# Rows for the next expert as quarter rows turned by VectorE, against half rows turned by TensorE

## The chip, the cores and the metric

The kernel runs on one core of a Trainium2 chip. The metric is the device time of one execution in microseconds (us). The profile names the engines PE (TensorE, matmuls), PEld (TensorE's weight loads), DVE (VectorE), ACT (ScalarE), POOL (GpSimd) and SP (SyncE, which here issues DMAs).

## The reference

Sliding-window attention over 8 sequences of 576 tokens with 8 heads of 64 gives a matrix x of 4608 rows and 512 columns, in float32. A two-level gate then sends each row to one of 4 groups and to one of 4 experts in it, and every expert is a small two-layer network:

```python
xg = x[mask_g]                                   # rows of one group
h  = np.maximum(xg[mask_e] @ w1[g, e], 0.0)      # 512 -> 1024
ye = h @ w2[g, e]                                # 1024 -> 512
out[tok_idx] = combined[:, None] * ye            # gate weights of group and expert
```

So the attention's rows are sorted by expert, multiplied by two weight matrices, scaled, and written to their places in the output.

## The kernel before, in words

**Stages.** Up to some 180 us of the profile the attention runs (`scores`, `softexp`, `transpose_p`, `av`), writes its rows to a DRAM tensor `xd` (L378), and counts, per token, the expert and the slot in it (`route`). A table `tab` (L569) holds for every slot the gate weight and the indices of the row in `xd` and in `out`; an index is doubled there since a row is fetched in two halves. From about 209 us on only the experts' networks run, one "piece" after the other (L1132). Pieces come in the order of the experts' counts; their row counts are `PIECES` (L41): 186 and 150 for the two experts part of whose rows was already done during the attention (`EARLY`, function `early`), then 368, 302, 300, 298, 292, 284, 266, 264, 256, 256, 242, 238, 214, 188. A tile is 128 rows, so pieces 2 to 9 have three tiles and the others two.

**One piece.** `ffn` yields after every step k. Steps 0 to 7 are `layer1`: for each 128 of the 1024 hidden units twelve matmuls into one PSUM buffer `a` (weights and rows are each split into two float16 parts, high and low, and three of the four products are taken), then ACT writes `hh` = relu(a) as float16 (L795) and DVE the rest `hl` (L796). Four PSUM buffers turn for `a`. From step 8 on is `layer2`: for each tile 24 matmuls into `y` (L847), two steps per tile, then ACT scales y (L821, or L831 for a short tile, whose columns are dealt to groups of partitions) and GpSimd scatters the rows to `out` by an indirect DMA (L808). The short tile comes second. A matmul takes `hh` and `hl` of the hidden units in order, so the last `hl` is wanted for the 22nd of the first tile's 24.

**Weights.** They come as 512 KB chunks, eight per expert, issued by SP (L659) into seven staging buffers. `split` (L666) turns each into two float16 parts: ACT the high one (L673), DVE the low one (L670). Four chunks of the expert after the next are split in `layer2` of a piece, the other four in `layer1` of the piece that follows.

**Rows of the next piece.** This is what the change touches. At the head of piece i, `begin(i + 1)` calls `slots_of` (L1095): DVE picks the piece's indices out of `tab` (`select`, L722 and L729, then `unpack`, L693 to L695), and `gather` (L750) lets GpSimd issue two indirect DMAs per tile (L738), each fetching half a row for each of 128 partitions into a tile `xr` (five buffers). After the gathers stands one `nc.gpsimd.drain()` (L1137). (Piece 2's are asked for in piece 0, L1147.) In `layer2` of piece i, `between` calls `spread` (L761) for one tile of piece i + 1 at a time: TensorE makes four transposes into PSUM (L769), ACT copies that as float16 into `xh` (L770), DVE subtracts for `xl` (L771). The transposes stand in TensorE's queue between the matmuls of `layer2`:

```python
for c in range(4):
    nc.tensor.transpose(pt[:, c, 0:n], xr[0:n, c * P : c * P + P], id32[0:n, 0:n])
nc.scalar.copy(xh[:, :, t * P : t * P + n], pt[:, :, 0:n])
nc.vector.tensor_tensor(xl[...], pt[:, :, 0:n], xh[...], ALU.subtract)
```

**Order.** In the attention and in the experts alike the order of the instructions of PE, ACT and DVE is that in which the program writes them (`manual_schedule`), in the experts POOL's and SP's too; each engine takes its own in that order. Between the attention and the first piece the string `TAIL` (L54) deals out steps by hand: R and r are steps of the last `route`, w one of the weights' preparation, 0, 1 and 2 steps of the three `early` passes, B the first piece's slots and gathers, O a step of `order`, which ranks the experts. `overflow` (L1020) makes a list of rows that found no slot, in 14 steps of DVE, dealt out by `bgq` from piece 3 on.

Of the kernel before, what the change touches and what calls it, by code (L numbers as in the profile page):

```python
# [38 lines left out]
CAPS = (442, 406, 368, 302, 300, 298, 292, 284, 266, 264, 256, 256, 242, 238, 214, 188)  # L39
DONE = [max([o + n for q, o, n, _ in EARLY if q == r] + [0]) for r in range(len(CAPS))]  # L40
PIECES = [(r, DONE[r], n - DONE[r]) for r, n in enumerate(CAPS)]  # L41
CGR = TPB * P // 4
CMAX = max(n for _, _, n in PIECES)
MAXOV = 64
NEARLY = 2
SPLITS = (2, 0, 2, 2, 2, 2, 2, 1, 1, 1, 1)
DEEP = 3
NWST = 6
NWST2 = 1
BUDGET = (1.4, 1.4, 2.4, 1.8)  # L50
# [17 lines left out]
def moe_attention_kernel(ctx, tc, q, k, v, cmask, wgate, wpack, out):  # L68
# [135 lines left out]
    def setup(part):  # L204
        if part == 0:
            nc.vector.memset(ones, 1.0)
            nc.gpsimd.affine_select(
                out=upper, in_=ones, pattern=[[1, P]], compare_op=ALU.is_gt, fill=0.0, base=0, channel_multiplier=-1
            )
            nc.sync.dma_start(wgr, wgate)  # L210
            iota_of(pri, [[-1, 4]], 4, 0)
            iota_of(base[0], [[REG, NE]], 0, 0)
            iota_of(low, [[1, P]], 0, 0)
        if part == 1:
            iota_of(high, [[REG // P, NE], [1, NK4]], 0, 0)
            nc.vector.tensor_scalar(high, high, float(P), HUGE, ALU.mult, ALU.add)
            nc.scalar.copy(high_ps, high.rearrange("p e k -> p (e k)"))
            nc.scalar.copy(pri_ps, pri)
            nc.vector.memset(E16, 0.0)
            nc.vector.memset(tab[:, 0], 0.0)  # L220
            nc.vector.memset(tab[:, 1], 2.0 * NTOK)
            nc.vector.memset(tab[:, 2], 2.0 * NTOK + 1.0)
            ids = wgr[:, 128:].rearrange("p (h v t) -> p h t v", h=2, v=2)
            nc.vector.tensor_copy(val[:, :, 1:3], ids[:, 0])
            nc.vector.tensor_copy(parts[:, :, 1:3], ids[:, 1])
        if part == 2:
            nc.gpsimd.memset(xe[0][0], 0.0)
            nc.sync.dma_start(xd[NTOK : NTOK + 1, :], xe[0][0][0:1, :])
        if part == 3:
            for g, t in oob.items():  # L230
# [459 lines left out]

    def unpack(ent, cs, three):
        n = three.shape[-1]
        nc.vector.tensor_copy(ent[:, 1:3, 0:n], three[:, 1:3])  # L693
# [23 lines left out]
        nc.scalar.copy(csq, rp[:, 1:2])  # L717
        return entq, csq

    def select(ent, cs, which, k0, nt):  # L720
        sq = sm.tile([P, 3, nt, NE], F32, name=f"sel{nt}")
        nc.vector.tensor_tensor(  # L722
            sq,
            tab[:, :, :, k0 : k0 + nt].rearrange("p v e k -> p v k e"),
            which.unsqueeze(1).unsqueeze(2).broadcast_to([P, 3, nt, NE]),
            ALU.mult,
        )
        three = sm.tile([P, 3, nt], F32, name=f"three{nt}")
        nc.vector.tensor_reduce(three, sq, axis=AX.X, op=ALU.add)  # L729
        unpack(ent, cs, three)  # L730
        return three

    def new_slots():
        return fs.tile([P, 3, 4], I32, name="sent"), fs.tile([P, 4], F32, name="cs")
# [15 lines left out]
    def gather(ent, cap):  # L750
        xrs = []
        for t, n in tiles(cap):
            xr = rows.tile([P, 512], F32, name="xr", bufs=5)
            fetch_rows(xr, ent, t)
            xrs.append(xr)
        return xrs

    def new_x(pl, cap=CMAX):
# [16 lines left out]
    more_a = [psS]  # L775

    def new_a():
        more_a.append(more_a.pop(0))
# [233 lines left out]
    def take(shape):  # L1012
# [4 lines left out]
        t = spare[:, lo : lo + n]  # L1017
        return t.rearrange("p (a b) -> p a b", a=shape[0]) if len(shape) > 1 else t

    def overflow():  # L1020
        T = lambda nm, shape: take(shape)
        cnt = T("cnt", [NE])
# [72 lines left out]
    def slots_of(i):  # L1095
        r, off, cap = pieces[i]
        ent, cs = new_slots()
        three = select(ent, cs, top[:, r] if r < NEARLY else perm[:, r], off // P, nt(cap))
        tq = note_tail(cs, three, cap)
        return ent, cs, gather(ent, cap), tq  # L1100

    def begin(i, got=None):
        ent, cs, xrs, tq = got or slots_of(i)
        return ent, cs, xrs, new_x(fx), tq

    cur = []

    def first(k):
        if 0 < k <= nt(pieces[0][2]):
            spread(cur[3], cur[2], pieces[0][2], (k - 1,))  # L1110

    def ready():
        cur[:] = begin(0)
# [5 lines left out]
    step = dict(R=lambda: part(lastr), r=lambda: run(lastr), w=lambda: run(wq), B=ready, O=lambda: run(rq))  # L1119
    step.update((str(i), lambda q=q: run(q)) for i, q in enumerate(eb))  # L1120
    for c in TAIL:
        step[c]()
# [5 lines left out]
    yq = [take([DM // 2]) for _ in range(2)]  # L1128
    for t in yq:
        nc.gpsimd.memset(t, 0.0)  # L1130
    ahead, sooner = [], []
    for i, (r, off, cap) in enumerate(pieces):  # L1132
        more = i + 1 < len(pieces)
        if more:
            nxt = begin(i + 1, sooner.pop() if sooner else None)
            ncap = pieces[i + 1][2]
            nc.gpsimd.drain()  # L1137
        nsel = nt(cap)

        def between(k):  # L1140
            m, d = nt(ncap), 2 * nsel - 2
            if more and k < d:
                spread(nxt[3], nxt[2], ncap, range(m * k // d, m * (k + 1) // d))
# [16 lines left out]
        if more:  # L1160
            cur = nxt
    run(bgq, 100)

    nov = nc.values_load(ovn[0:1, 0:1], min_val=0, max_val=MAXOV)
# [26 lines left out]
def layout(q, k, v, moe_w_group, moe_w_expert, moe_w1, moe_w2):  # L1191
# [70 lines left out]
```

## Time and profile before

| | us |
|---|---|
| three runs | 580.63, 582.28, 584.22 |
| median of them | 582.28 |
| the profiled execution | 584.71 |
| its span, first to last instruction | 583.0 |
| from the first matmul of piece 0 to the first of piece 15 | 351.34 |

The trace belongs to the profiled execution, which took 2.43 us more than the median. A stretch of it is named by its start and end in us from the span's start. "Busy" of PE is modelled, since matmuls are pipelined; where PE is called busy all the time, the distance from one matmul's start to the next one's tells what it costs. DVE's and ACT's durations overlap by some 0.07 us where two instructions follow each other at once.

### The profile page before, as it was taken

The numbers are of one execution on the slowest core, as the hardware profiler recorded it, in microseconds if no ns is written. First come the engines' busy times: TensorE is split into PE (matmuls) and PEld (weight loads), VectorE is DVE, ScalarE is ACT, GpSimd is POOL, SyncE is SP. The second block draws the span as 40 slices with busy tenths as digits, with TensorE's granted clock in tenths as the row PEclk, the third lists the DMA queues.
The fourth block names the chain that finished last, engine by engine and source line by source line (L and its number), as shares of the span: only waits on it lengthen the run. The fifth ranks groups of instructions, "written<-read, shape, count | busy, mean of one in ns | idle before, by whom it ended". The sixth has DMA issues, their size and how long they took to land.

```text
span 583.0 us, 16256 instructions
## 1 busy us (share of the span) xinstructions
PE 553.9 (95%) x6460; PEld 396.0 (68%) x6460; DVE 386.1 (66%) x801; ACT 331.4 (57%) x656; POOL 248.5 (43%) x275
## 2 busy tenths in 40 slices
PE   3989999897899999999999999999999999999995
PEld 2777877675767777656666666675766766776873
DVE  5756987889688636855877876565655756756720
ACT  7456685865766427744455555555466656555521
POOL 2885675647464342342343425151541422332411
PEclk9899999999799999999999999999999999999999
DMA  7999898993772176875667566576856767867210
GB/s 236 347 295 294 297 289 260 313 326 102 245 264 91 56 290 217 264 254 166 195 206 229 188 203 216 188 240 202 267 185 225 241 229 234 277 221 247 82 30 31
DMA packets 45344, 127.41 MB, mean 219 GB/s; under 512 B 6845, under 2 KB 7747, under 8 KB 45266
## 3 DMA queue, kind: packets, MB, share of 16 engines
q1 hardware_dynamic: 37506, 105.36, 56.2%
q0 software_dynamic: 7760, 20.99, 10.2%
q8 instruction: 52, 0.85, 0.6%
q14 instruction: 26, 0.21, 0.1%
HBM read 107.44 MB, written 19.22 MB: 217 GB/s over the span
## 4 chain that ended last, share of the span: by engine, by line
PE 69%; issue 2%; DVE 1%; DMA 1%; POOL 1%; ACT 1%; POOLq 0%; SPq 0%
PE y L847 32%; PE a L788 31%; PE pt L769 3%; DMA w<-wpack 1%; DVE mv L534 0%; PE o L331 0%; PE lt_ps L406 0%; PE tx L392 0%; POOL out L808 0%; PE rp L714 0%; PE bank L553 0%; POOL xe L979 0%; DVE wa2l L670 0%; POOL vs L152 0%; ACT wa2h L673 0%
## 5 line engine op out<-in xcount | busy, mean ns | idle before, releaser
L738 POOL DMA_INDIRECT xr<-xd,sent x80 | 95.2, 1190 | 32.6 <-issue 21.5
L808 POOL DMA_INDIRECT out<-yr,sent x30 | 30.9, 1029 | 179.4 <-ACT yr L821 148.5
L847 PEld LDWEIGHTS <-hh 128*128 128x128 f16 (+14 forms) x960 | 67.1, 99 | 57.7 <-issue 2.7
L796 DVE SCALAR_TENSOR_TENSOR hl<-a,hh 128x256 f16<-128x256 f32 (+14 forms) x136 | 56.9, 421 | 62.6 <-ACT hh L795 62.5
L795 ACT ACTIVATE hh<-a 128x256 f16<-128x256 f32 (+14 forms) x136 | 51.5, 383 | 49.7 <-PE a L788 49.0
L788 PE MATMUL a<-xh,wb1h 128*128 128x256 f16 (+7 forms) x288 | 76.7, 270 | 0.0
L788 PE MATMUL a<-xh,wb1l 128*128 128x256 f16 (+7 forms) x288 | 76.6, 270 | 0.0
L788 PE MATMUL a<-xl,wb1h 128*128 128x256 f16 (+7 forms) x288 | 76.6, 270 | 0.0
L771 DVE TENSOR_TENSOR xl<-pt,xh 128x512 f16<-128x512 f32 (+14 forms) x42 | 24.6, 589 | 74.2 <-ACT xh L770 74.2
L821 ACT ACTIVATE yr<-y,cs 128x512 f32<-128x512 f32 (+4 forms) x30 | 20.6, 687 | 88.9 <-PE y L847 59.6
L788 PE MATMUL a<-xh,wa1h 128*128 128x186 f16 (+7 forms) x256 | 70.8, 277 | 0.0
L788 PE MATMUL a<-xh,wa1l 128*128 128x186 f16 (+7 forms) x256 | 70.7, 277 | 0.0
L788 PE MATMUL a<-xl,wa1h 128*128 128x186 f16 (+7 forms) x256 | 70.7, 277 | 0.0
L788 PEld LDWEIGHTS <-wa1h 128*128 128x128 f16 x640 | 59.6, 99 | 11.6 <-issue 0.5
L788 PEld LDWEIGHTS <-wb1h 128*128 128x128 f16 x576 | 54.2, 98 | 9.6 <-issue 0.2
L847 PE MATMUL y<-wb2h,hh 128*128 128x512 f16 (+7 forms) x272 | 59.7, 305 | 0.0
L847 PE MATMUL y<-wb2l,hh 128*128 128x512 f16 (+7 forms) x272 | 59.6, 304 | 0.0
L847 PE MATMUL y<-wb2h,hl 128*128 128x512 f16 (+7 forms) x272 | 59.5, 304 | 0.0
L847 PE MATMUL y<-wa2h,hh 128*128 128x512 f16 (+7 forms) x208 | 56.8, 331 | 0.0
L847 PE MATMUL y<-wa2h,hl 128*128 128x512 f16 (+7 forms) x208 | 56.6, 330 | 0.0
L847 PE MATMUL y<-wa2l,hh 128*128 128x512 f16 (+7 forms) x208 | 56.6, 330 | 0.0
L148 POOL TENSOR_SCALAR vs<-v 64x1040 f32<-64x1040 f32 x36 | 38.7, 1088 | 30.2 <-DMA v<-v 18.5
(206 smaller groups left out, 1255.0 us busy)
## 6 DMA issues: line engine op xcount, KB each, us to landing
w<-wpack SPq DMA_DIRECT2D x128, 512.0 KB, 4.1
v<-v SPq DMA_DIRECT2D x36, 260.0 KB, 5.5
kr<-k SPq DMA_DIRECT2D x34, 256.0 KB, 5.4
qb<-q SPq DMA_DIRECT2D x17, 512.0 KB, 6.0
xd<-x SPq DMA_DIRECT2D x32, 256.0 KB, 4.3
xr<-xd,sent POOLq DMA_INDIRECT x80, 4.1
xd<-x SPq DMA_DIRECT2D x8, 128.0 KB, 4.0
qb<-q SPq DMA_DIRECT2D x2, 256.0 KB, 2.8
```

Source lines behind the costliest of these rows:

```text
L148: nc.gpsimd.tensor_scalar(vs[n][even], vt[n][even], 1.0, 1.0, ALU.mult, ALU.mult)
L738: nc.gpsimd.indirect_dma_start(out=xr[:, 256 * h : 256 * h + 256], out_offset=None, in_=xd[0:known].rearrange("n (h c) -> (n h) c", h=2), ...
L769: nc.tensor.transpose(pt[:, c, 0:n], xr[0:n, c * P : c * P + P], id32[0:n, 0:n])
L771: nc.vector.tensor_tensor(xl[:, :, t * P : t * P + n], pt[:, :, 0:n], xh[:, :, t * P : t * P + n], ALU.subtract)
L788: nc.tensor.matmul(a[:, 0:cap], ww[:, c * FF + f * P : c * FF + f * P + P], xx[:, c, 0:cap], start=(i == 0), stop=(i == len(mm) - 1),)
L795: nc.scalar.activation(hh[:, f, 0:cap], a[:, 0:cap], AF.Relu)
L796: nc.vector.scalar_tensor_tensor(hl[:, f, 0:cap], a[:, 0:cap], 0.0, hh[:, f, 0:cap], ALU.max, ALU.subtract)
L808: ins = nc.gpsimd.indirect_dma_start(out=out.rearrange("n (g c) -> (n g) c", g=g), out_offset=bass.IndirectOffsetOnAxis(ap=at, axis=0), in ...
L821: nc.scalar.activation(yr[0:n, :], yp[0:n, :], AF.Copy, scale=cs[0:n, t : t + 1])
L847: nc.tensor.matmul(yp[P // g * j : P // g * j + n, 0 : DM // g], h[:, f, t * P : t * P + n], ww[:, f * DM + DM // g * j : f * DM + DM // g ...
```

## The change

Each row of `xd` is now seen as four quarters of 128 columns. For 32 rows of a tile, one indirect DMA fetches all four quarters: partitions 32j to 32j + 31 receive quarter j of the 32 rows. A full tile takes four such DMAs, a shorter one as many as it has groups of 32 rows. DVE then turns 32x32 blocks (`spread_quarters`) into a tile `xt` in SBUF, and ACT and DVE make `xh` and `xl` from it. With this the row's column 4p + c stands on partition p in chunk c, so the first weight matrix is laid out anew on the host, and the tiles that TensorE still transposes (the `early` ones and piece 0) read every fourth column.

The quarter rows' indices come from a second table, made once by sixteen small matmuls and one DVE instruction (`quarter_table`, Q in `TAIL`); `quarter_rows` picks a piece's indices from it. A tile at a time is asked for, at every odd step, as long as fewer than five tiles are held, up to three pieces ahead (`ask_ahead`); G and H in `TAIL` ask for piece 1 and for the first tile of piece 2. The turns come at steps 3, 5, 7 and 9. The DRAIN stands at step 5. `overflow` gets only steps divisible by four.

```diff
-    "R0rw00rrrrrrrrrrrw1rrrr0rr1r1rr11rrr1rrB1w12w1ww112w22ww2w2O2O2O2O2O2O"
-    "222"
+    "R0rw00rrrrrrrrrrrw1rrrr0rr1r1rr11rrr1rrB1w1Q2w1Gww112w22ww2w2O2O2O2O2O2O"
+    "222H"
...
+    def quarter_table():
+        ps = new_a()[:, 0 : 4 * NE * NK4].rearrange("p (t n) -> p t n", t=4)
+        for T in range(4):
+            for j in range(4):
+                nc.tensor.matmul(
+                    ps[Q4 * j : Q4 * j + Q4, T],
+                    id32[:, Q4 * T : Q4 * T + Q4],
+                    tab[:, 1 + j // 2].rearrange("p e k -> p (e k)"),
+                    start=True,
+                    stop=True,
+                )
+        tabq.append(take([4, NE * NK4]))
+        nc.vector.tensor_scalar(tabq[0], ps, 2.0, odd, ALU.mult, ALU.add)
+
+    def quarter_rows(which, k0, nt):
+        sq = qsq[:, 0 : 4 * nt * NE].rearrange("p (k t e) -> p k t e", k=nt, t=4)
+        nc.vector.tensor_tensor(
+            sq,
+            tabq[0].rearrange("p t (e k) -> p k t e", k=NK4)[:, k0 : k0 + nt],
+            which.unsqueeze(1).unsqueeze(2).broadcast_to([P, nt, 4, NE]),
+            ALU.mult,
+        )
+        at = qat[:, 0 : 4 * nt].rearrange("p (k t) -> p k t", k=nt)
+        nc.vector.tensor_reduce(at, sq, axis=AX.X, op=ALU.add)
+        entq = fs.tile([P, 4, 4], I32, name="sentq")
+        nc.vector.tensor_copy(entq[:, 0:nt], at)
+        return entq
...
+    def gather_quarters(entq, cap, xrs):
+        def tile_of(t, n):
+            xr = rows.tile([P, 4, P], F32, name="xr", bufs=NXR)
+            for T in range((n + Q4 - 1) // Q4):
+                nc.gpsimd.indirect_dma_start(
+                    out=xr[:, T],
+                    out_offset=None,
+                    in_=xd.rearrange("n (g c) -> (n g) c", g=4),
+                    in_offset=bass.IndirectOffsetOnAxis(ap=entq[:, t, T : T + 1], axis=0),
...
+    def spread_quarters(xs, xrs, cap):
+        turned = []
+        for t, n in tiles(cap):
+            m = (n + Q4 - 1) // Q4
+            xt = rows.tile([P, 4, 4, Q4], F32, name="xt")[:, 0:m]
+            nc.vector.transpose(xt, xrs[t][:, 0:m].rearrange("p t (d c) -> p t c d", c=4))
+            held_rows[0] -= 1
+            turned.append((t, m, xt))
+            if t:
+                halves_of(xs, *turned.pop(0))
+            yield
+        halves_of(xs, *turned.pop(0))
+        yield
+
+    def halves_of(xs, t, m, xt):
+        xt = xt.rearrange("p t c j -> p c t j")
+        h, l = (x[:, :, t * P : t * P + m * Q4].rearrange("p c (t j) -> p c t j", j=Q4) for x in xs)
+        nc.scalar.copy(h, xt)
+        nc.vector.tensor_tensor(l, xt, h, ALU.subtract)
...
+            xq = xr.rearrange("p (d c) -> p c d", c=4)
             for c in range(4):
-                nc.tensor.transpose(pt[:, c, 0:n], xr[0:n, c * P : c * P + P], id32[0:n, 0:n])
+                nc.tensor.transpose(pt[:, c, 0:n], xq[0:n, c], id32[0:n, 0:n])
...
+    def ask_ahead(i):
+        if held_rows[0] < NXR:
+            if known[-1][4]:
+                ask(1, known[-1])
+            elif len(known) < min(i + 4, len(pieces)):
+                known_next(1)
...
-        more = i + 1 < len(pieces)
-        if more:
-            nxt = begin(i + 1, sooner.pop() if sooner else None)
-            ncap = pieces[i + 1][2]
-            nc.gpsimd.drain()
+        nxt, turn = None, []
+        if i + 1 < len(pieces):
+            while known[i + 1][4]:
+                ask(1, known[i + 1])
+            nxt = begin(known[i + 1])
+            turn = [spread_quarters(nxt[3], nxt[2], pieces[i + 1][2])]
         nsel = nt(cap)
-
-        def between(k):
-            m, d = nt(ncap), 2 * nsel - 2
-            if more and k < d:
-                spread(nxt[3], nxt[2], ncap, range(m * k // d, m * (k + 1) // d))
-
-        for k, _ in enumerate(ffn(wsets[r % 2], cur[3], cur[0], cur[1], cap, new_h, between, cur[4])):
-            if i == 0 and k == 1:
-                sooner.append(slots_of(2))
+        for k, _ in enumerate(ffn(wsets[r % 2], cur[3], cur[0], cur[1], cap, new_h, tq=cur[4])):
+            if k % 2:
+                ask_ahead(i)
+                if k == 5:
+                    nc.gpsimd.drain()
+                if k > 2:
+                    run(turn)
...
-            elif r > NEARLY:
+            elif r > NEARLY and k % 4 == 0:
                 run(bgq)
...
-    w1 = np.asarray(moe_w1).reshape(NE, 4, P, FF).transpose(0, 2, 1, 3).reshape(NE, P, 4 * FF)
+    w1 = np.asarray(moe_w1).reshape(NE, P, 4 * FF)
```

## Rows read from the trace of the kernel before

**Rows 1.** The page, busy time of the engines over the span.

```profile
PE 553.9 (95%) x6460; PEld 396.0 (68%) x6460; DVE 386.1 (66%) x801; ACT 331.4 (57%) x656; POOL 248.5 (43%) x275
```

**Rows 2.** The chain of work that ended last, 209.16 to 560.50 us, by line.

```profile
by line: PE y L847 48.8%; PE a L788 46.0%; PE pt L769 4.8%; PE rp L714 0.5%
```

**Rows 3.** Busy time by stretch: all pieces but the last, piece 1, piece 8.

```profile
core 0: us, PE busy (x) PEld busy (x) DVE busy (x) ACT busy (x) POOL busy (x), PEclk, DMA share, GB/s
209.16:560.50 351.34, 351.34 (x2967) 239.47 (x2966) 227.58 (x424) 196.65 (x334) 125.01 (x110) 1.00 0.67 217
...
225.86:240.31 14.45, 14.45 (x237) 11.31 (x237) 10.76 (x19) 11.25 (x22) 2.00 (x2) 1.00 0.92 301
...
406.44:430.97 24.53, 24.53 (x262) 16.61 (x261) 15.06 (x28) 14.48 (x26) 10.80 (x9) 1.00 0.69 227
```

**Rows 4.** Timeline of PE in piece 4: start, duration, instruction, count.

```profile
317.16 0.38 PE L847 MATMUL y<-wa2l,hh 128*128 128x512 f16 x1
317.38 0.60 PE L769 MATMUL pt<-id,xr 128*128 128x128 f32 x4
317.91 0.29 PE L847 MATMUL y<-wa2h,hh 128*44 128x256 f16 x2
...
319.13 0.27 PE L847 MATMUL y<-wa2l,hh 128*44 128x256 f16 x2
319.33 0.66 PE L769 MATMUL pt<-id,xr 128*128 128x128 f32 x4
319.92 0.29 PE L847 MATMUL y<-wa2h,hh 128*44 128x256 f16 x2
...
321.13 0.28 PE L847 MATMUL y<-wa2l,hh 128*44 128x256 f16 x2
321.34 0.44 PE L769 MATMUL pt<-id,xr 42*128 42x42 f32 x4
321.71 0.39 PE L847 MATMUL y<-wa2h,hh 128*128 128x512 f16 x1
```

**Rows 5.** DVE's groups by shape: count, busy us, mean ns, idle before.

```profile
L670 DVE SCALAR_TENSOR_TENSOR wb2l<-w,wb2h 128x1024 f16<-128x1024 f32 x32 | 38.8, 1216 | 0.0
...
L771 DVE TENSOR_TENSOR xl<-pt,xh 128x512 f16<-128x512 f32 x28 | 19.2, 689 | 56.9 <-ACT xh L770 56.9
...
L796 DVE SCALAR_TENSOR_TENSOR hl<-a,hh 128x266 f16<-128x266 f32 x8 | 3.4, 431 | 3.7 <-ACT hh L795 3.7
...
L722 DVE TENSOR_TENSOR sel<-tab,perm 128x144 f32<-128x144 f32 x8 | 3.2, 405 | 0.0
...
L796 DVE SCALAR_TENSOR_TENSOR hl<-a,hh 128x150 f16<-128x150 f32 x8 | 2.2, 306 | 1.3 <-ACT hh L795 1.3
...
L722 DVE TENSOR_TENSOR sel<-tab,perm 128x96 f32<-128x96 f32 x6 | 1.9, 319 | 0.0
...
L722 DVE TENSOR_TENSOR sel<-tab,top 128x48 f32<-128x48 f32 x2 | 0.5, 230 | 0.0
```

**Rows 6.** TensorE, transposes' weight loads (ns), and a row of the chain.

```profile
L769 PEld LDWEIGHTS pt<-id,xr x160: 133/140/143, 202.7 to 554.9; 128*128 128x128 f32 x104, 58*128 58x128 f32 x4, 22*128 22x128 f32 x4, 112*128 112x128 f32 x4
...
158.26 1.02 PE o L331 x32
```

**Rows 7.** Gathers and scatters: groups, landing, and two gathers beside one DVE instruction.

```profile
L738 POOL DMA_INDIRECT xr<-xd,sent x80: 992/1044/2052, 180.8 to 547.9; - x80
...
DMA to landing us min/median/max: 2.7/4.1/6.3
...
L808 POOL DMA_INDIRECT out<-yr,sent x30 | 30.9, 1029 | 179.4 <-ACT yr L821 148.5 <-ACT xh L770 15.2 <-DVE tq L706 4.3
...
306.13 1.00 POOL L738 DMA_INDIRECT xr<-xd,sent  x1 [0.30 <-issue]
307.44 1.64 POOL L738 DMA_INDIRECT xr<-xd,sent  x1 [0.30 <-issue]
...
306.99 1.22 DVE L670 SCALAR_TENSOR_TENSOR wb2l<-w,wb2h 128x1024 f16<-128x1024 f32 x1
```

**Rows 8.** Timeline of DVE at the end of piece 1.

```profile
239.33 1.22 DVE L771 TENSOR_TENSOR xl<-pt,xh 128x512 f16<-128x512 f32 x2 [2.44 <-ACT xh L770]
```

More of the change, by code (lines that the diff above doesn't have):

```diff
@@ L41 @@
 PIECES = [(r, DONE[r], n - DONE[r]) for r, n in enumerate(CAPS)]
+Q4 = P // 4
 CGR = TPB * P // 4
@@ L47 @@
 DEEP = 3
+NXR = 5
 NWST = 6
@@ L184, in moe_attention_kernel @@
     capt = cp.tile([P, NE], F32, name="capt")
+    odd = cp.tile([P, 1], F32, name="odd")
     top = cp.tile([P, NEARLY, NE], F32, name="top")
@@ L692, in unpack @@
         n = three.shape[-1]
-        nc.vector.tensor_copy(ent[:, 1:3, 0:n], three[:, 1:3])
+        if three.shape[1] == 3:
+            nc.vector.tensor_copy(ent[:, 1:3, 0:n], three[:, 1:3])
         nc.vector.tensor_scalar(ent[:, 0, 0:n], three[:, 1], 0.5, 0.0, ALU.mult, ALU.add)
@@ L718, in tail_slots, with select @@
         return entq, csq
-    def select(ent, cs, which, k0, nt):
-        sq = sm.tile([P, 3, nt, NE], F32, name=f"sel{nt}")
+    def select(ent, cs, which, k0, nt, nv=3):
+        sq = sm.tile([P, 3, nt, NE], F32, name=f"sel{nt}")[:, 0:nv]
         nc.vector.tensor_tensor(
             sq,
-            tab[:, :, :, k0 : k0 + nt].rearrange("p v e k -> p v k e"),
-            which.unsqueeze(1).unsqueeze(2).broadcast_to([P, 3, nt, NE]),
+            tab[:, 0:nv, :, k0 : k0 + nt].rearrange("p v e k -> p v k e"),
+            which.unsqueeze(1).unsqueeze(2).broadcast_to([P, nv, nt, NE]),
             ALU.mult,
         )
-        three = sm.tile([P, 3, nt], F32, name=f"three{nt}")
+        three = sm.tile([P, 3, nt], F32, name=f"three{nt}")[:, 0:nv]
         nc.vector.tensor_reduce(three, sq, axis=AX.X, op=ALU.add)
@@ L752, in gather @@
         for t, n in tiles(cap):
-            xr = rows.tile([P, 512], F32, name="xr", bufs=5)
+            xr = rows.tile([P, 512], F32, name="xr", bufs=NXR)
             fetch_rows(xr, ent, t)
@@ L756, in gather, with new_x @@
         return xrs
-    def new_x(pl, cap=CMAX):
+    def gather_quarters(entq, cap, xrs):
[7 more added lines that the diff above has]
+                    in_offset=bass.IndirectOffsetOnAxis(ap=entq[:, t, T : T + 1], axis=0),
+                    bounds_check=4 * NTOK + 3,
+                    oob_is_err=False,
+                )
+            xrs.append(xr)
+        return [lambda t=t, n=n: tile_of(t, n) for t, n in tiles(cap)]
+    def spread_quarters(xs, xrs, cap):
[16 more added lines that the diff above has]
+        nc.vector.tensor_tensor(l, xt, h, ALU.subtract)
+    def new_x(pl, cap=(CMAX + Q4 - 1) // Q4 * Q4):
         return pl.tile([P, 4, cap], F16, name="xh"), pl.tile([P, 4, cap], F16, name="xl")
@@ L1018, in take @@
         return t.rearrange("p (a b) -> p a b", a=shape[0]) if len(shape) > 1 else t
+    qsq, qat = take([4 * 3 * NE]), take([4 * 3])
     def overflow():
@@ L1097, in slots_of, with ask, begin, known_next @@
         ent, cs = new_slots()
[L1098 to L1103, printed above, removed]
-        return ent, cs, xrs, new_x(fx), tq
+        which = top[:, r] if r < NEARLY else perm[:, r]
+        xrs, asks = [], []
+        if i:
+            asks = gather_quarters(quarter_rows(which, off // P, nt(cap)), cap, xrs)
+            three = select(ent, cs, which, off // P, nt(cap), 2)
+        else:
+            three = select(ent, cs, which, off // P, nt(cap))
+            xrs = gather(ent, cap)
+        return ent, cs, xrs, note_tail(cs, three, cap), asks
+    def ask(n, got):
+        for _ in range(min(n, len(got[4]))):
+            got[4].pop(0)()
+            held_rows[0] += 1
+    def begin(got):
+        ent, cs, xrs, tq, _ = got
+        return ent, cs, xrs, new_x(fx), tq
+    known = []
+    def known_next(n):
+        known.append(slots_of(len(known)))
+        ask(n, known[-1])
+    def ask_ahead(i):
[4 more added lines that the diff above has]
+                known_next(1)
     cur = []
@@ L1110, in first @@
             spread(cur[3], cur[2], pieces[0][2], (k - 1,))
+            held_rows[0] -= 1
     def ready():
-        cur[:] = begin(0)
+        known.append(slots_of(0))
+        held_rows[0] = nt(pieces[0][2])
+        cur[:] = begin(known[0])
     lastr = [route(NBP - 1)]
@@ L1118, in moe_attention_kernel @@
     eb.append([early(2, new_x(fx), new_h, first)])
-    step = dict(R=lambda: part(lastr), r=lambda: run(lastr), w=lambda: run(wq), B=ready, O=lambda: run(rq))
+    step = dict(R=lambda: part(lastr), r=lambda: run(lastr), w=lambda: run(wq), B=ready, O=lambda: run(rq), Q=quarter_table)
+    step.update(G=lambda: known_next(9), H=lambda: known_next(1))
     step.update((str(i), lambda q=q: run(q)) for i, q in enumerate(eb))
@@ L1157, in moe_attention_kernel @@
                 todo.pop(0)()
-            elif r > NEARLY:
+            elif r > NEARLY and k % 4 == 0:
                 run(bgq)
-        if more:
-            cur = nxt
+        while run(turn, 9):
+            pass
+        cur = nxt
     run(bgq, 100)
```

7 lines of the change are left out of this document (5 added, 2 removed).

## The prediction

> **What bounds the kernel now.** I read the page's busy times first, then the chain of waits of the experts' stretch, then stretches, then single instructions. On the page PE is busy 95% of the span, DVE 66%, ACT 57%, POOL 43% [rows 1]. An average over two different stages says little, so: from the first matmul of piece 0 to the first of piece 15 PE is busy all of 351.34 us, at a granted clock of 1.00, DVE 227.58 (65%), POOL 125.01 (36%), and the 16 DMA engines 0.67 [rows 3]. The chain there holds PE alone: layer 2 48.8%, layer 1 46.0%, the transposes of the next piece's rows 4.8% [rows 2]. No other engine's wait ends last. So in this stretch one us of TensorE's time taken away is one us gained, as long as what replaces it keeps up.
>
> **What the change removes.** The transposes of pieces 1 to 15: two tiles for piece 1, three each for pieces 2 to 9, two each for 10 to 15, so 38 tiles. The chain's share gives 0.048 x 351.34 = 16.9 us [rows 2], 0.44 per tile. Starts of matmuls show the whole price. A 512-column matmul takes 0.216 (512 columns at the 2.4 GHz level); with the transposes between, the next starts 317.91 - 317.16 = 0.75 later, so they cost 0.53. The second set costs 0.79 - 0.11 = 0.68, the third, of 42 rows, 0.58 - 0.11 = 0.47 [rows 4]; 1.68 for a piece where the chain counts 0.53 + 0.59 + 0.37 = 1.49. The difference is time that the chain books on the matmul before a transpose. By that ratio 16.9 becomes about 19.0. I take 18.0, between 16.9 and 19.0.
>
> **What it adds on TensorE.** (a) Sixteen matmuls of 64 columns with 32 output partitions, after the table is done. The nearest row: 32 float32 matmuls of that width and 130 columns take 1.02 us, four side by side [rows 6]; sixteen are 0.5. Below: 0.25 by columns. Above: one after another at a transposes' set's 0.53 per four, 2.1. I take 0.5. (b) The transposes that stay (four early tiles, two of piece 0, 24 weight loads) now read every fourth column, 16 bytes apart. No row shows TensorE reading so. Below: nothing. Above: as DVE's strided read, priced next, 0.7 x 0.140 [rows 6] x 24 = 2.4. I take the middle, 1.2.
>
> **What it adds on DVE.** No row shows a 32x32 turn. Contiguous rows: 512 elements take 689 ns, 266 take 431, so 1.05 ns per element and some 0.15 us besides [rows 5]. L722 reads its table at a step of 16 bytes: 48, 96 and 144 elements take 230, 319 and 405 ns, so 1.8 ns per element [rows 5]. The turn reads at the same step. A full tile thus takes 0.69 to 1.07 us; I take the upper end, since the access is the same. Groups of 32 rows: piece 1 has 5, piece 2 has 12, pieces 3 to 6 have 10 each, 7 to 9 have 9 each, 10 to 13 have 8 each, 14 has 7, 15 has 6: 129, or 16,512 elements. At 1.8 ns that is 30 us, with 0.15 for each of 38 tiles 35; at 1.05, 23.
>
> The Trainium skill weighs on this: its page "SBUF — State Buffer", section "Door 1: The DMA port swizzle", says that SBUF is read in 16-byte lines and that each access that goes to a new line pays. L722 agrees (1.8 against 1.05) [rows 5]. The page does not say which engine pays; if TensorE's weight loads do, its rule gives the 2.4 us of (b) and 1.2 us more than my sum, if not, 1.2 less.
>
> The index pick per piece grows: a product of 192 elements instead of 144 (0.5 against 0.4), a reduction and a cast more, a third of the old select less: some 0.7 us, 10 for 15 pieces. `xl`'s subtraction reads SBUF instead of PSUM with the same count, so 0.69 as before [rows 5]. DVE's 227.58 becomes 261 to 273 of some 333 us, 82% at most: it is not the bound over the stretch.
>
> Inside a piece it can be. Piece 8 (266 rows): layer 1 takes eight times 12 x 0.113 = 10.9 us, and the last `hl` is wanted after 21 more matmuls of 0.216, 15.4 us from the start. In DVE's queue up to it stand 8 `hl` (0.36 from start to start), four weight splits (1.14), a step of the overflow list (1.4), two turns (0.6 to 1.0) and one subtraction (0.6): 10.7 to 11.5, from 1.8 us on, done at 12.5 to 13.3. There are 2 us to spare, and four buffers of `a` let DVE lag by three steps before.
>
> Piece 1 is the tight one: 150 rows, 14.45 us with 0.43 + 0.91 of transposes in it, 13.1 without, and piece 2's three long tiles to be made ready in it. Already in the run before, the third `xl` ends at 239.33 + 1.22 = 240.55 [rows 8], as piece 2 begins at 240.31 [rows 3]. Then DVE has up to that point 8 `hl` (0.25 from start to start; 0.306 each alone [rows 5]) 2.0, five splits 5.7, three turns 2.0 to 3.2, three subtractions 1.8, and piece 4's index pick 1.6: 13.1 to 14.3, from 1.2 us on, so it ends at 14.3 to 15.5. TensorE waits 1.2 to 2.4 us, once. I take 1.8. With nothing in front (DVE idle, pick later) it is 0; with a turn at twice my price 5.
>
> **What it moves.** GpSimd: 76 gathers become 129, each of 128 pieces of 512 bytes, 8.5 MB instead of 10.0. A gather takes 1.04 us (0.99 to 2.05) and 0.30 passes to the next; a scatter 1.03 [rows 7]. A piece with ten gathers and three scatters: 13 x 1.34 = 17.4 us of 25.5; if all gathers meet a DVE split (1.64 instead of 1.00 [rows 7]) 23.4 of 25.5. Each tile is asked for at least some eight steps before its turn, over 10 us, and lands in 4.1 [rows 7]. Queued behind a gather are the scatters; with two buffers of `y` rows one may be some 10 us late before ACT waits. The DRAIN stands behind a gather before and after; nothing visible waits for it, so 0. On DMA, 16,512 pieces instead of 9,728 make at most a few hundredths on 0.67 [rows 3]. ACT copies from SBUF instead of PSUM, the same count: 0. The overflow list's steps come later, beside matmuls: 0.
>
> **The sum**, against the profiled execution's 584.7: -18.0 + 0.5 + 1.2 + 1.8 = -14.5, so 570.2. The median of the runs shown is 2.4 below that execution, so 567.8, **568 us**, 2.5% faster. Ends of its terms: -19.0 + 0.25 + 0 + 0 gives 563.5, and -16.9 + 2.1 + 2.4 + 5 gives 574.9.
>
> **Rivals.** (1) DVE gives part back in every piece: a turn waits for its gather or takes 2 us instead of 1, and `hl` comes late. The margin in piece 8 is 2 us, so turns of 2.1 use it up; a wait of 0.6 us beyond it in each of 13 pieces makes 568 + 8 = 576. For: the turn is in no row. Against: 2 us of margin. (2) The turn is so slow that DVE is the bound: that needs 333 - 227.6 - 10 = 95 us for 38 tiles, 2.5 us each, over twice the strided price; near it, stalls give most of 18 us back: 582. (3) Slower: POOL becomes the bound. In the stretch there are 36 scatters at 1.33 and some 120 gathers. It would be as long as today at (351 - 48) / 120 = 2.52 us per gather, its 0.30 included; that is the point from which it decides. The longest row is 2.05 + 0.30 = 2.35. If each gather met two of DVE's two-input instructions, 1.00 + 2 x 0.64 + 0.30 = 2.58, and the requests of a piece also stood one us behind the turn that frees their buffer, 15 x 1 + 120 x 2.58 + 48 = 373, 22 us over today's 351: 604. For: the change makes `xl` another instruction with two SBUF inputs. Against: the median gather is at 1.04.
>
> The Trainium skill backs the third's mechanism: "SBUF — State Buffer", section "Who interferes with whom", has such a DVE instruction and a GpSimd one that reads SBUF exclude each other. The trace agrees, 1.64 beside a split against 1.00 [rows 7].
>
> (4) The change doesn't do what it says: the transposes go, but something else ends last already, as a weight chunk. Against: no such wait in the chain [rows 2]; DMA at 0.92 in piece 1 [rows 3] for it. Then 580.
>
> **How the numbers follow.** The forecast 0.70, (1) 0.14, (2) 0.05, (3) 0.07, (4) 0.04. About 1% can be told from no change, that is 576.5 and 588.1. Faster by over 1%: 0.70 and 0.11 of (1), 0.81. Within: 0.03 of (1), 0.05 of (2), 0.04 of (4) and 0.01 of (3), 0.13. Slower by over 1%: 0.06 of (3). For eight in ten I take the forecast from a little below its low end, 562.5, and most of (1), up to 577.5.
>
> **What would show it.** Right: L769 with 24 instead of 176 matmuls; PE busy without a gap from piece to piece but for one of 1 to 2.4 us before piece 2; piece 4's length shorter by 1.7 us; turns of 0.7 to 1.1 us per tile; gathers still near 1.0 to 1.7 us; POOL's busy share under 65% in the stretch. Wrong: matmuls of layer 2 waiting for L796, or of layer 1 for `xl`, in every piece; turns above 2 us; gathers above 2.2 us; a fall of the granted clock where such gaps stand.

## The result and the profile after

The changed kernel takes 586.6 us (median of 12 runs, 583.56 to 589.05), the kernel before in the same session 582.22 (579.85 to 584.22). The ratio is 1.0073, with a 95% interval of 1.0050 to 1.0096: a little slower, by some 4 us, where 568 had been forecast. The profiled execution took 587.25 us, its span is 585.5.

The page of the changed kernel: busy times, then the granted clock in 40 slices, then the chain that ended last, by engine.

```profile
PE 542.3 (93%) x6340; PEld 381.8 (65%) x6340; DVE 425.6 (73%) x870; ACT 332.2 (57%) x656; POOL 329.5 (56%) x332
...
PEclk9999999999999999789999999999998999999999
...
PE 53%; issue 6%; DVE 6%; DMA 4%; POOL 3%; ACT 2%; POOLq 1%; SPq 0%; DVEq 0%; ACTq 0%
```

Against [rows 1], PE has 120 instructions fewer and is busy 11.6 us less, but in a span that is 2.5 us longer. TensorE no longer bounds every stretch: in the chain of the experts' stretch, which held PE alone before [rows 2], DVE, DMA and POOL now appear. The clock dips at 234 to 263 us and at 439 to 454, in a stretch where it was 1.00 before [rows 3].

Stretches of the changed kernel, the counterparts of [rows 3]: all pieces but the last; piece 1; piece 2. The columns are as there.

```profile
207.28:563.50 356.22, 339.19 (x2813) 225.25 (x2812) 264.70 (x485) 197.57 (x334) 202.68 (x162) 0.98 0.65 211
...
223.29:246.12 22.83, 13.55 (x226) 10.02 (x225) 14.20 (x30) 10.99 (x22) 13.27 (x13) 0.91 0.59 188
246.12:280.33 34.21, 33.02 (x168) 17.96 (x168) 24.24 (x36) 17.38 (x27) 22.10 (x17) 0.91 0.68 211
```

The stretch is 356.22 us instead of 351.34, and TensorE idles in 17.0 of it. Piece 1 alone took 14.5 before; now it takes 22.83, with TensorE busy 13.55. By pieces, from the start of each one's first matmul in the two timelines of PE:

| pieces | before, us | after, us | difference |
|---|---|---|---|
| 0 | 16.80 | 16.01 | -0.8 |
| 1 | 14.52 | 22.83 | +8.3 |
| 2 | 31.99 | 34.21 | +2.2 |
| 3 to 7, together | 133.97 | 126.49 | -7.5 |
| 8 | 24.54 | 24.29 | -0.3 |
| 9 | 24.08 | 28.60 | +4.5 |
| 10 to 14, together | 105.44 | 103.79 | -1.7 |

(In [rows 3] the window of piece 1 begins 0.07 us after its first matmul, hence 14.45 there.) So where nothing stops TensorE, the gain is there: 1.5 us in each of pieces 3 to 7. It is given back in pieces 1, 2 and 9, and in smaller parts in 8, 11 and 12: in run 5 below, where nothing stops TensorE there, piece 8 takes 23.06 us and pieces 10 to 14 together 101.24.

The turns and gathers themselves, the changed kernel's groups by line (count, busy us, mean ns, idle before) and the weight loads of the transposes that stayed (shortest, median, longest ns):

```profile
L798 POOL DMA_INDIRECT xr<-xd,sentq x124 | 152.8, 1232 | 93.3 <-issue 38.7 <-DVE sel L728 22.8 <-DVE xT L764 6.1
...
L815 DVE STREAM_TRANSPOSE xt<-xr 128x512 f32<-128x512 f32 (+3 forms) x38 | 36.6, 962 | 0.0
...
L842 PEld LDWEIGHTS pt<-id,xr x8: 192/209/214, 200.7 to 204.4; 128*128 128x128 f32 x4, 58*128 58x128 f32 x4
```

What stops TensorE is to be read at the end of piece 1, backwards from PE. Four timelines of the changed kernel (start, duration, engine, line; in brackets the idle time before and what ended it). PE:

```profile
236.84 0.27 PE L920 MATMUL y<-wb2l,hh 128*22 128x128 f16 x4
246.12 0.47 PE L861 MATMUL a<-xh,wa1h 128*128 128x368 f16 x1 [9.01 <-ACT xh L827]
247.78 0.47 PE L861 MATMUL a<-xl,wa1h 128*128 128x368 f16 x1 [1.19 <-DVE xl L828]
```

ACT, with the end of piece 0's first tile and the copy that PE waits for:

```profile
220.70 0.69 ACT L894 ACTIVATE yr<-y,cs 128x512 f32<-128x512 f32 x1 [2.85 <-issue]
...
245.45 0.62 ACT L827 CAST xh<-xt 128x512 f16<-128x512 f32 x1 [9.13 <-DVE xt L815]
```

DVE:

```profile
236.28 0.25 DVE L735 TENSOR_REDUCE three<-sel 128x6 f32<-128x96 f32 x1
243.89 0.17 DVE L700 TENSOR_SCALAR sent<-three 128x3 int32<-128x3 f32 x1 [7.36 <-DMA out<-yr,sent]
...
244.34 1.08 DVE L815 STREAM_TRANSPOSE xt<-xr 128x512 f32<-128x512 f32 x1
```

POOL:

```profile
227.37 1.03 POOL L798 DMA_INDIRECT xr<-xd,sentq  x1 [0.30 <-issue]
228.71 1.00 POOL L798 DMA_INDIRECT xr<-xd,sentq  x1 [0.30 <-issue]
235.80 0.99 POOL L798 DMA_INDIRECT xr<-xd,sentq  x1 [6.09 <-DVE xT L764]
...
239.70 1.00 POOL L798 DMA_INDIRECT xr<-xd,sentq  x1 [0.30 <-issue]
241.00 1.03 POOL L881 DMA_INDIRECT out<-yr,sent  x1 [0.31 <-issue]
```

Read from the end: the first matmul of piece 2 waits for `xh`, that for the third turn, and the turn stands in DVE's queue behind L700. L700 writes the slot table `sent` of piece 4. The pool of tables has four buffers, and with the look-ahead of the change five pieces are known in piece 1, so the buffer is that of piece 0, which its scatter still reads. That scatter's data were ready at 220.70 + 0.69 = 221.39, but it was issued at 241.00: 19.6 us late. In that time GpSimd did what stood in front of it in its queue, ten gathers, and idled 6.1 us once. The profile puts the end of this idle time down to DVE. Another row of the same trace, the one for the line of the DRAIN, says otherwise (sequencer, count, shortest, median, longest ns, first and last start), for the window 215 to 228 us:

```profile
L1247 POOLq DRAIN  x1: 13743/13743/13743, 221.2 to 221.2; - x1
```

From 221.2 to 234.9 the sequencer sits in the DRAIN, and 0.9 us later the next gather begins. The same pattern in piece 9 gives its 4.5 us. Over the run DVE's queue waits for scatters 18.5 us, the changed kernel's view of waits (us in total, times, longest):

```profile
DVE sent L700 <- DMA out<-yr,sent: 18.5, 6, 7.4
...
PE a L861 <- ACT xh L827: 9.0, 1, 9.0
...
PE a L861 <- DVE hl L869: 5.4, 3, 3.8
PEld L920 <- DVE hl L869: 3.9, 5, 1.1
```

### The profile page after: what moved, and what is told of

The parts are those of the page before. It is cut to its first block, busy times and chain, and to the rows that moved or that the text cites. A ratio compares the mean times of both kernels' runs of the same rounds, so it can differ in the third digit from the quotient of the medians.

```text
span 585.5 us, 16199 instructions
## 1 busy us (share of the span) xinstructions
PE 542.3 (93%) x6340; PEld 381.8 (65%) x6340; DVE 425.6 (73%) x870; ACT 332.2 (57%) x656; POOL 329.5 (56%) x332
## 4 chain that ended last, share of the span: by engine, by line
PE 53%; issue 6%; DVE 6%; DMA 4%; POOL 3%; ACT 2%; POOLq 1%; SPq 0%; DVEq 0%; ACTq 0%
PE a L861 26%; PE y L920 25%; DMA out<-yr,sent 3%; POOL xr L798 2%; DVE wb2l L675 1%; POOL out L881 1%; DMA w<-wpack 1%; DVE hl L869 1%; DVE xt L815 1%; DMA xr<-xd,sentq 1%; DVE xl L828 1%; DVE mv L539 0%; POOLq L1247 0%; DVE wa1l L675 0%; DVE wa2l L675 0%
## 5 line engine op out<-in xcount | busy, mean ns | idle before, releaser
L798 POOL DMA_INDIRECT xr<-xd,sentq x129 | 160.3, 1243 | 95.0 <-issue 40.0
L881 POOL DMA_INDIRECT out<-yr,sent x30 | 40.2, 1340 | 66.1 <-ACT yr L894 47.5
L861 PEld LDWEIGHTS <-wa1h 128*128 128x128 f16 x640 | 59.5, 99 | 22.9 <-issue 12.5
L920 PEld LDWEIGHTS <-hl 128*128 128x128 f16 (+14 forms) x480 | 34.3, 99 | 29.9 <-DVE hl L869 3.9
```

What stands on the lines that cost most here:

```text
L798: nc.gpsimd.indirect_dma_start(out=xr[:, T], out_offset=None, in_=xd.rearrange("n (g c) -> (n g) c", g=4), in_offset=bass.IndirectOffsetOn ...
L861: nc.tensor.matmul(a[:, 0:cap], ww[:, c * FF + f * P : c * FF + f * P + P], xx[:, c, 0:cap], start=(i == 0), stop=(i == len(mm) - 1),)
L881: ins = nc.gpsimd.indirect_dma_start(out=out.rearrange("n (g c) -> (n g) c", g=g), out_offset=bass.IndirectOffsetOnAxis(ap=at, axis=0), in ...
L920: nc.tensor.matmul(yp[P // g * j : P // g * j + n, 0 : DM // g], h[:, f, t * P : t * P + n], ww[:, f * DM + DM // g * j : f * DM + DM // g ...
```

## The experiments

The theory to test, A: scatters are issued late, behind gathers and the DRAIN, and DVE stops because a slot table that it wants to write is still read by one. Rivals: the DRAIN acts through late gathers (B); the DRAIN costs nothing (B'); DVE just has too much to do in the tight pieces (C). To compare runs without the stage ahead of the pieces, whose length varied between 205.0 and 209.7 us among these kernels without being touched by their edits, I give three terms from each trace: from the first matmul of piece 0 to the last matmul (S), TensorE's idle times of 0.3 us and more in it (I), and what follows to the span's end (E). Before: S 367.6, I 0, E 6.4. Changed: S 372.5, I 16.3, E 5.7.

**1. Eight slot tables** (e1_ring8).

```diff
-    fs = pool("fs", 4, reuse_waits="tile")
+    fs = pool("fs", 8, reuse_waits="tile")
```

> The changed kernel with one size different: the pool of slot tables (`sent`, `cs`, `sentq`, `tq`) has 8 buffers instead of 4. Its DVE waits 18.5 us, in six waits, for a scatter to land before it can write `sent` (L700), the longest 7.36 us, and TensorE idles 9.0 + 1.2 us at the end of piece 1, 3.8 in piece 9 and 2.3 in smaller gaps. Theory A (the table of the piece three ahead shares a buffer with the piece whose scatters are still queued, so DVE stops in its queue and its turns, `xl` and `hl` come late): these waits go, piece 1's gap falls to 1 to 3 us and piece 9's to under 1, the clock falls less, the run takes 571 to 577 us. Rival B (the DRAIN inside the piece is what costs, through late gathers and scatters): L700 no longer waits, but a turn (L815) waits for its gather instead, and 582 to 587 remain. Rival C (DVE has simply too much to do in pieces 1 and 9): gaps stay within 1 us, 585 to 588.

Measured: 579.83 us, ratio 0.9958 (0.9929 to 0.9987). S 364.1, I 8.1, E 6.1. The wait at L700 is gone and piece 1's idle time fell from 10.2 to 3.0 us; that much of A holds, and C falls. But the time stayed above A's range, for a new wait in piece 3, timelines of ACT and PE of this run:

```profile
283.05 0.69 ACT L894 ACTIVATE yr<-y,cs 128x512 f32<-128x512 f32 x1 [12.08 <-DMA out<-yr,sent]
```

```profile
285.55 0.41 PE L861 MATMUL a<-xh,wb1h 128*128 128x302 f16 x1 [4.75 <-DVE hl L869]
```

ACT could not write `yr`, of which there are two: the same late scatters, read through another ring. `hh` and `hl` stood behind it in the queues of ACT and DVE.

**2. No DRAIN** (e2_no_drain).

```diff
-                if k == 5:
-                    nc.gpsimd.drain()
```

> The changed kernel without its DRAIN on GpSimd, nothing else. In the changed kernel GpSimd idles 4.5 to 6.1 us once per piece between two gathers (229.71 to 235.80 in piece 1), with the scatters of the piece queued behind. Theory A with the DRAIN as the root: these idle stretches go, the scatters are issued about 5 us earlier, so the DVE waits for scatters fall from 18.5 us to under 5, piece 1's gap from 9.0 to 2 to 5 us, and the time is 571 to 579. Rival B' (the idle stretches are waits for the buffers that the turns free, or for the index pick on DVE, and the DRAIN costs nothing): they stay at 4 us or more and the time stays at 584 to 588.

Measured: 587.44 us, ratio 1.0117 (1.0054 to 1.0180). S 365.4, I 11.0, E 12.6. A's range was missed by 8 us at least, for two reasons that the trace shows; the time lies in the range of B', but not for the reason that B' gives. First, the idle time in front of the scatter went, but the gathers stayed. Its `yr` was ready at 220.18 and it was issued at 234.73, ten gathers later, as POOL's timeline shows:

```profile
231.51 1.55 POOL L798 DMA_INDIRECT xr<-xd,sentq  x1 [0.30 <-issue]
233.37 1.05 POOL L798 DMA_INDIRECT xr<-xd,sentq  x1 [0.30 <-issue]
234.73 1.13 POOL L881 DMA_INDIRECT out<-yr,sent  x1 [0.31 <-issue]
```

So L700 still waited, 12.7 us in five times instead of 18.5 in six. Second, S became 7.1 us shorter, and E 6.9 us longer: the gain was lost after the last matmul. B' falls in piece 1, where the idle time of 6.1 us was the DRAIN's. In later pieces idle times of 4 to 6 us stayed, as B' says: there GpSimd waits for picks and turns anyway.

**3. Both edits** (e3_ring8_no_drain).

> Both edits: 8 buffers of slot tables and no DRAIN. If the two are one chain (DRAIN, late scatter, DVE's wait), this is within 2 us of the better of the two alone, 569 to 574 us, which is the forecast of 568 nearly reached. If each costs by itself, the gains add. If DVE's work is the limit (rival C), gaps of 1 us and more stay in pieces 1, 9 and 12 and the time is above 580.

Measured: 575.59 us, ratio 0.9910 (0.9876 to 0.9943). S 353.5, I 3.3, E 12.7. Here the stretch is as good as forecast, 14.1 us shorter than before, with the 1.7 + 1.3 us before piece 2 as the only larger idle times. The traced execution is the fastest of ten, though: 573.10 us at a granted clock of 0.991 over the run, where the others go up to 579.88 at 0.977. What is lost in the trace is lost at the end: the last scatter is issued at 559.57 and the span ends at 571.3, 11.7 us later; in the changed kernel it is 585.5 - 580.77 = 4.7. The line with the span, and the last scatter in the timeline of POOL:

```profile
core 0 of [0], span 571.3 us
...
559.57 0.98 POOL L881 DMA_INDIRECT out<-yr,sent  x1 [3.95 <-ACTq L1266]
```

**4. The DRAIN behind the piece's last scatter** (e4_drain_at_end).

```diff
-                if k == 5:
-                    nc.gpsimd.drain()
...
         while run(turn, 9):
             pass
+        nc.gpsimd.drain()
         cur = nxt
```

> The changed kernel with its DRAIN put behind the piece's last scatter instead of between the gathers of the piece (at step 5); same number of DRAINs. Theory A with the DRAIN as the root: what counts is only what is queued behind it; here the next scatter is a piece's length away, the next gathers have over 10 us to spare, so the time is within 2 us of the run without the DRAIN, 571 to 579. Rival: the DRAIN holds GpSimd until all DMAs have landed wherever it stands, and the next piece's gathers become late: turns (L815) wait for gathers and the time stays at 583 to 590.

Measured: 589.38 us, ratio 1.0125 (1.0070 to 1.0180). S 371.0, I 14.7, E 7.8. A miss for my reading that only what is queued right behind it counts. GpSimd is some ten gathers behind the other engines there, so a DRAIN after the last scatter of piece 0 comes in front of work that is already due: 238.00 + 1.00 to 244.73, and piece 1's scatter at 254.70, as POOL's timeline shows.

```profile
238.00 1.00 POOL L881 DMA_INDIRECT out<-xT,entq  x1 [0.31 <-issue]
244.73 1.28 POOL L798 DMA_INDIRECT xr<-xd,sentq  x1 [5.73 <-DVE xl L828]
...
254.70 1.03 POOL L881 DMA_INDIRECT out<-yr,sent  x1 [0.30 <-issue]
```

DVE's waits for scatters stay at 17.0 us. The time lies in the rival's range, but its cause is not there: no turn waits for a gather. There were two questions left: whether every ring that a late scatter reads has to be deeper, and what the DRAIN does for the end.

**5. Eight slot tables and four `yr`, all DRAINs in place** (e5_ring8_rows4). The two buffers more are row buffers that lie unused by then.

```diff
-    fs = pool("fs", 4, reuse_waits="tile")
+    fs = pool("fs", 8, reuse_waits="tile")
...
-    ycnt = [0]
+    ycnt, more_y = [0], [None]
...
-            yr = rows.tile([P, 512], F32, name="yr")
+            more_y.append(more_y.pop(0))
+            yr = rows.tile([P, 512], F32, name="yr") if more_y[-1] is None else more_y[-1]
...
+    more_y[:] = [xe[0][0], None, xe[1][0], None]
     ahead = []
```

> The changed kernel with every DRAIN in its place, 8 buffers of slot tables, and four buffers of scaled y rows (`yr`) instead of two. With the deeper table ring alone the wait had moved: ACT could not write `yr` (L894) for 12.08 us (to 283.05) because the scatter two tiles earlier was still queued, hh and hl stood behind it, and TensorE idled 4.75 us at 280.8. Theory A' (the scatters are late in GpSimd's queue, behind gathers and the DRAIN, and what costs is every ring whose buffer a late scatter still reads): with both rings deeper nothing waits for a scatter, only the 1.7 + 1.3 us before piece 2 remain, and the time is 571 to 576 although GpSimd works exactly as slowly as before. Rival (late gathers are the next thing to end last, since the DRAIN holds them too): turns (L815) wait for gathers, 578 to 584.

Measured: 571.12 us, ratio 0.9794 (0.9759 to 0.9828). S 356.4, I 3.0, E 6.2. This settles it: GpSimd works as late as in the changed kernel, with the DRAIN's idle time in front of the same scatter, and the rings alone take 15.5 us off. In POOL's timeline of this run:

```profile
229.25 1.00 POOL L798 DMA_INDIRECT xr<-xd,sentq  x1 [0.30 <-issue]
235.79 0.99 POOL L798 DMA_INDIRECT xr<-xd,sentq  x1 [5.55 <-DVE hl L869]
...
241.47 1.46 POOL L881 DMA_INDIRECT out<-xe,sent  x1 [0.30 <-ACT wb1h L678]
```

B falls: this run's view of waits has no turn that waits for a gather.

**6. Eight slot tables and one DRAIN, in the last piece** (e6_ring8_one_drain).

```diff
-                if k == 5:
+                if k == 5 and i + 1 == len(pieces):
```

> 8 buffers of slot tables, two of `yr`, and a single DRAIN, in the last piece, where GpSimd idles 9.6 us before its last tail scatter. Without any DRAIN the span ended 11.7 us after the last scatter was issued, with one per piece 4.7. Theory D (the DRAINs do a clearing up of finished requests, which without them is left for the end of the program): one late DRAIN, hidden in that idle time, takes the 7 us back, so 566 to 571 from 575.6. Rival (the 7 us at the end are something else, or a DRAIN for all requests at once takes over 10 us itself): 574 to 578.

Measured: 570.22 us, ratio 0.9785 (0.9755 to 0.9815). S 356.4, I 2.9, E 6.4. One DRAIN, between the gathers that are long done and the last tail scatter, takes E from 12.7 back to 6.4. It lasts 11.0 us (its row for the line), and the scatter that it could hold up goes out 0.8 us after its data are ready:

```profile
L1247 POOLq DRAIN  x1: 10993/10993/10993, 547.7 to 547.7; - x1
```

**7. Look-ahead one piece shorter, four tables, DRAINs in place** (e7_look_ahead_3).

```diff
-            elif len(known) < min(i + 4, len(pieces)):
+            elif len(known) < min(i + 3, len(pieces)):
```

> The changed kernel with the look-ahead cut by one piece (at most two pieces ahead of the next are known), 4 buffers of slot tables, DRAINs in their place. The table that a new pick overwrites is then that of a piece whose scatters had a whole piece more to land. Theory A: DVE's waits for scatters (L700, 18.5 us) go without a deeper ring; ACT's wait for a `yr` buffer may come in their place as with 8 buffers; 575 to 581. If asking later starves the turns (rival: the look-ahead was needed), L815 waits for gathers and the time is 585 to 592.

Measured: 575.74 us, ratio 0.9888 (0.9850 to 0.9926). S 358.2, I 5.6, E 6.1. As A says: no wait at L700 is left with four tables, since the buffer is now that of a piece further back, and ACT's wait for a `yr` buffer (9.6 us, once, in piece 3) comes in its place.

**8. The kernel before without its DRAIN** (e8_before_no_drain).

```diff
-            nc.gpsimd.drain()
```

> The kernel before without its DRAIN. My prediction put its DRAIN at nothing. Theory D: nothing changes inside the run (no wait there ends at GpSimd), but the end of the program grows by the 7 us that the changed kernel without DRAIN showed, or by less, as it has 76 gathers instead of 129 (some 4 to 5 us): 585 to 589. Rival: the DRAIN costs nothing and does nothing in this kernel: 581 to 583.

Measured: 583.85 us, ratio 1.0024 (1.0004 to 1.0044). S 367.6, I 0, E 8.6. The stretch is the same to 0.1 us, so in the kernel before the DRAIN did cost nothing, and the end grew by 2.2, which is less than I expected and more than the rival says. That its price could be seen before the change is shown by rows of the kernel before that I had not read for the prediction: the DRAINs' own row, over the run and in the window 300 to 320 us, and the timeline of POOL there.

```profile
L1137 POOLq DRAIN  x15: 7848/8994/11704, 190.0 to 543.5; - x15
...
L1137 POOLq DRAIN  x1: 11207/11207/11207, 303.9 to 303.9; - x1
...
309.38 1.65 POOL L738 DMA_INDIRECT xr<-xd,sent  x1 [0.30 <-issue]
318.59 1.03 POOL L808 DMA_INDIRECT out<-yr,sent  x1 [7.56 <-ACT yr L821]
```

It ends at 303.9 + 11.2 = 315.1, about 4.1 us after the last gather, and the next thing for GpSimd is due at 318.5. There were 3.5 us to spare.

**9. Two DRAINs per piece** (e9_two_drains).

```diff
-                if k == 5:
+                if k in (3, 5):
```

> The changed kernel with a second DRAIN per piece (at step 3 as well as step 5), buffers as they are: the suspected cost doubled. Theory A': a DRAIN keeps GpSimd from its next request until the requests before it have landed, so a second one pushes the scatters back by up to 5 us more where the queue is full (pieces 0 to 2); DVE's waits for scatters (18.5 us) and ACT's grow and the time is 589 to 597. Rival (the second one finds nothing more to wait for, since GpSimd was going to idle anyway for picks and turns): 585 to 588.

Measured: 612.74 us, ratio 1.0499 (1.0426 to 1.0573). S 394.9, I 31.2, E 6.0. Twice the DRAINs add 26 us, more than A's range: the scatter of piece 0 goes out at 247.37, and DVE's longest wait for one grows from 7.4 to 11.8 us.

```profile
DVE sent L700 <- DMA out<-yr,sent: 31.1, 7, 11.8
...
ACT yr L894 <- DMA out<-yr,sent: 11.0, 1, 11.0
```

**10 and 11. Both rings deeper with one DRAIN, without and with the shorter look-ahead** (e10_rings_one_drain, e11_rings_one_drain_look_3): the edits of 5 and 6, and of 5, 6 and 7.

> Both rings deeper (8 slot tables, four `yr`) and a single DRAIN in the last piece. Nothing waited for a scatter any more with the deeper rings and all DRAINs (571.1 us) nor with 8 tables and one DRAIN (570.2). Theory A': the two cures are for the same waits and do not add, 569 to 571.5. Rival (DRAINs also cost where no ring shows it, through the gathers): 565 to 568.

> As the run with both rings deeper and one DRAIN, and a look-ahead of one piece less, so that the index pick of piece 4 (1.6 us of DVE) no longer stands in piece 1. What is left there is 1.7 + 1.3 us of idle TensorE before piece 2, which I had priced at 1.8, and a granted clock of 0.72 behind it, which makes piece 2 some 3 us longer (34.9 against 32.0 where the clock did not fall). With the pick gone the idle time falls to 1 to 1.6 us as in the run with the look-ahead alone (0.5 + 1.0); if the clock holds, 565 to 568, the forecast; if it falls again, 568 to 570. If the shorter look-ahead starves the turns instead, gaps of 1 to 2 us come at pieces 1 and 3 (as 1.4 and 2.3 in that run) and the time stays at 570 to 574.

Measured: 570.69 us, ratio 0.9807 (0.9773 to 0.9841), S 356.4, I 3.0, E 6.5; and 569.58 us, ratio 0.9794 (0.9752 to 0.9836), S 353.4, I 2.9, E 6.1. The cures don't add, as A says. The shorter look-ahead halves the idle time right before piece 2 (0.5 + 1.0), but 1.4 us come in layer 1 of piece 1, so I is the same; what differs is the clock in piece 2. Stretches of piece 2, run 10 and then run 11:

```profile
237.09:272.01 34.92, 33.58 (x169) 18.25 (x169) 24.21 (x36) 17.37 (x27) 28.52 (x22) 0.90 0.75 228
```

```profile
238.87:270.54 31.67, 30.67 (x176) 17.23 (x169) 23.72 (x36) 17.27 (x27) 21.93 (x17) 1.00 0.79 253
```

The expectation of 565 to 568 for a clock that holds was missed by 1.6 us; in the profiled executions the stage ahead of the pieces, which none of these edits touches, began them 1.5 us later than in run 10. By the intervals the two can't be told apart. All of runs 5, 6, 10 and 11 are about 2% faster than the kernel before.

## Why the prediction was wrong

**What held.** The transposes' price: over all pieces but the last, run 11 takes 544.32 - 207.18 = 337.1 us, with 2.9 of idle time, 334.2, against 351.3 before, so 17.1 us; I had 18.0, between the chain's 16.9 and 19.0 by ratio. Pieces 3 to 7 show which of the two views was right: 1.50 each, the chain's 1.49, not the 1.68 from matmul starts, for three tiles. A turn takes 1.09 us in the median (1.07 taken for a full one), DVE's 264.7 us in the stretch lie in the 261 to 273, a gather's median is 1.02 us, and GpSimd is busy 57% of the stretch. The idle time before piece 2 that DVE's own work makes is 3.0 us in run 5, where no wait for a scatter is left (1.8 taken from 1.2 to 2.4, 5 as its upper end). So rivals 1 and 2 fall as they were put, for the turns are not slow, and so does 3: the mean of 1.23 and 0.30 us is far from 2.52, though one gather took 6.1. Two of the signs of being wrong did come, for another cause: `hl` was late in pieces 8, 9, 11 and 12, and the granted clock fell where the gaps stand.

Of the rule in the Trainium skill's page "SBUF — State Buffer", section "Door 1: The DMA port swizzle", that an access which goes to a new 16-byte line pays, I had left open whether TensorE's weight loads pay. Here they do: 209 ns in the median against 140 [rows 6], which is 24 x 0.069 = 1.7 us of loads; as the stage with most of them varied by 4.7 us, what that is worth in the sum is not shown.

**What failed** is one step, in two sentences: "The DRAIN stands behind a gather before and after; nothing visible waits for it, so 0", and "with two buffers of `y` rows one may be some 10 us late before ACT waits". I priced GpSimd as a rate: 17.4 of 25.5 us for a piece of ordinary length, so below its limit. But it is a queue in program order, and in pieces 0 and 1, which last only 16.0 and some 14 us, the change puts requests for pieces 2 and 3 into it ahead of the scatters, with a DRAIN among them. Then the scatter of piece 0 is 19.6 us late: ten gathers at 1.35 us are 13.5, the DRAIN 6.1. Before, the DRAIN stood behind the last gather with 3.5 us to spare; now gathers and scatters stand right behind it, and the same instruction costs.

The second half of the step is that I asked only one ring, that of `yr`, whether it bears a late scatter. A scatter also reads its slot table, and the same change makes that ring tight: in piece i the tables up to that of piece i + 3 are written, where before it was that of piece i + 1 (in piece 0 also piece 2's). DVE, which writes the table in its queue between turns, stops. The prediction has this very write in piece 1, as "piece 4's index pick 1.6", but as work of DVE and not as something that can wait; it waited 7.4 us. I did not list what each moved DMA reads and who writes that buffer next.

From there the account closes: 334.2 us at the full clock without idle time, 17.0 us of idle time, and a remainder of 5.0 us, where the granted clock is below 1.00 and for which the sum had no term, make 356.2; the pieces' stretch is 4.9 us longer than before, the rest of the span 2.4 shorter. Run 5 shows that with both rings deeper and nothing else changed the forecast's mechanism gives its gain; its 571.1 lies 3 us above 568. In its trace the span is 12.5 us below that of the kernel before, where the sum had 14.5. Three terms were worse: 17.1 for 18.0 of transposes, 3.0 for 1.8 of waiting before piece 2, and 3.0 for the clock in piece 2 (34.95 us, against 32.0 in run 3), which was not priced. The part outside the stretch, where the sum had 1.7 us more for the sixteen matmuls and the strided transposes, came out 1.4 shorter; as the stage ahead of the pieces varies by 4.7 us, what these two are worth stays open.

What was not tried is to issue the scatters ahead of the gathers that are not yet due, and four `yr` with four tables.

## What to carry to other kernels

Price an in-order DMA queue by position, not by its busy share: for the first pieces write down what stands in front of each request, and when its data are ready. For every request that becomes later, list the buffers that it reads, how deep their rings are and which engine writes them next; that engine's whole queue stops with it. A synchronising instruction that costs nothing while no request behind it is due has a duration of its own in the trace; read it before other work is put behind it.

## What the runs showed of the hardware

- The GpSimd DRAIN lasts 7.8 to 11.7 us by its own rows in the kernel before, 3.9 to 13.7 in the changed one; it spans requests still being issued, and lets the next one go some 4 to 6 us after the last, where the gathers' median time to land is 3.6 us. That it waits for the landing is an inference from these two numbers.
- Without any DRAIN the span ends 11.7 us after the last scatter's issue instead of 4.7 (changed kernel), 7.6 instead of 5.4 (kernel before); a single DRAIN that is over 10.7 us before the span's end (547.7 + 11.0 against 569.4) brings it to 5.4. What is cleared up in it no trace shows.
- The same idle time in front of piece 2 (1.6 to 1.7 and 1.3 us) was followed by a granted clock of 0.90 over the piece in run 10 (a mean of the levels 1.2 and 2.4 GHz) and of 1.00 in run 3, which is 3 us. Executions of one kernel differ as well, with the clock over the run: those of run 5 go from 568.59 us at 0.994 to 572.26 at 0.983, the traced one. So it need not be the kernels that differ here; why the clock falls in one and not in another is open.
